# Attention steps emitted in another order

## The chip, the cores and the metric

The kernel runs on one core of a Trainium2 chip. Its time is the device time of one execution in microseconds (us); the span is the part of it between the first and the last recorded instruction. TensorE (PE in the profile) multiplies matrices and, in a queue of its own, loads weights (PEld); VectorE (DVE), ScalarE (ACT) and GpSimd (POOL) work on tiles; SyncE (SP) issues most of the transfers. Each engine runs its own instructions in the order in which the program emits them, and semaphores between engines make it wait.

## The reference

Four batches, eight heads, 768 positions of 64 numbers. Each query and each key is assigned to the nearest of 16 centroids of its head, and attention runs only inside a cluster. The result (3072 tokens of 512) is routed by a greedy choice among eight experts of capacity 384, each a two-layer network:

```
q_assign = argmax(normalize(q) @ normalize(c).T);  k_assign likewise
scores = where(q_assign == k_assign, q @ k.T / 8, -1e9)
x = softmax(scores) @ v
logits = x @ w_gate            # 3072 x 8
# greedy over all (token, expert) pairs by falling logit:
# a token takes an expert that still has room (384 tokens each)
out[tokens of e] = relu(x[tokens of e] @ w1[e]) @ w2[e]
```

## The kernel before

The attention works on eight units, a batch and four heads each; u below is the unit. In a unit there are 24 key tiles s of 128 rows (four heads of six). The steps of a unit, with the lines that record them:

- `load` brings q, k, v (L497, SP). `split_sc`, `split_hi` (ScalarE, L648, L652) and `split_lo` (GpSimd or VectorE, L659, L657) scale a tile and write it as a sum of two half-precision parts. `trans` (L740) has a DMA transpose it. Unit 0 is split and transposed head by head, with `pt` (TensorE, L746) and `ptc` (VectorE L752 or ScalarE L750), which needs no transfer.
- `c0`, `c1`, `c2` to `c4` (L528 to L559) normalise the centroids: squares on VectorE, a root on ScalarE (`c1`, L531), a chain of eleven short VectorE steps, a transpose and a copy. `cent` (L671) multiplies by them, and `hot` or, in unit 0, `hh` (L693 to L709) make a one-of-16 code of the largest product, the last step on ScalarE.
- `m_mm` (L788) and `m_rd` (VectorE, L792) make the maximum of one key tile's scores over a whole row; `row0`, `row1` (GpSimd), `rowt` and `row2` (SP, L813, L817) put the negative maxima into the transposed code of q, so that the score step subtracts them.
- `b_mm` (L827 and L831, four matmuls into one of three score buffers) makes the scores with the cluster term, `b_exp` (ScalarE, L834) their exponentials, and `res` (L842, mostly GpSimd) what the exponential loses in half precision. Four pairs of buffers hold exponentials and residuals.
- `av` (L853 to L859) multiplies exponentials and residuals with v, 18 matmuls, for the six tiles of a head into one accumulator. `out0` to `out2` divide (VectorE, L863 to L877), `hi0` (ScalarE, L885) and `hi1` (VectorE, L889) copy the head out, and the next head's `av` needs the accumulator free. `xst` stores it, `xtr` or, in the last unit's second half, `xpt` and `xpc` transpose it, and `lg0` to `lg2` (L921 to L935) add it to the router's logits.
- `bb,x,i` and `bq,x` (VectorE, L1045 to L1066) start the routing of the first three (x = 0) and the last quarter of the tokens; `bq` writes 128 threshold comparisons (L1063). 86 `tab` steps (mostly GpSimd, L965 to L975) fill small constant tables that only the routing needs. `wd` (L678) is a matmul whose result nobody reads.

All this is written out under a manual schedule: `ATT_ORDER` is a text with one word for each step, and `steps_of` reads it. Steps are emitted in that order; what an engine does first is therefore settled by the text alone, and a step waits only for the buffers and values that it needs. A second text, `FFN_ORDER`, does the same for the experts; the routing between the two texts (L1175 on, with its first decision at L1243) is plain code. The loop is:

```
for name, args in steps_of(ATT_ORDER):
    ...
        norm2[args[0]]()
        hots(int(name[3]), *args)
        hots0(int(name[2]), *args)
        FN[name](*args)
```

Of the kernel before, what the change touches and what calls it, by code (L numbers as in the profile page):

```python
# [26 lines left out]
hh4,0,k zqb split_sc,0,k,3 load,0,v,- split_hi,0,k,1,P split_lo,0,k,1,P pt,0,ka,1 ptc,0,ka,1,D pt,0,qa,3 ptc,0,qa,3,D
pt,0,qa,2 split_hi,0,k,3,P split_lo,0,k,3,P split_hi,0,k,2,P pt,0,ka,3 split_sc,0,v,- split_hi,0,v,-,P zkb ptc,0,qa,2,D
hh5,0,k pt,0,kb,0 ptc,0,ka,3,D ptc,0,kb,0,D cent0,1,k cent0,1,q hh0,1 hh1,1 dup,0,q,0 hh5,0,q dup,0,k,3 pt,0,qb,0
split_lo,0,k,2,P pt,0,ka,2 hh2,1 dup,0,q,1 hh3,1 hh4,1,q dup,0,k,2 hh4,1,k ptc,0,qb,0,A m_mm,0,3 m_rd,0,3 m_mm,0,4  # L30
split_lo,0,v,-,P m_rd,0,4 ptc,0,ka,2,A m_mm,0,5 m_rd,0,5 hh5,1,q dup,0,k,1 load,1,v,- split_sc,1,v,- vs,0 vh2,0 vact,0 vl2,0
load,1,k,- split_sc,1,k,- tab,0 m_mm,0,2 m_rd,0,2 cent0,2,k cent0,2,q hh0,2 hh1,2 tab,31 hh2,2 pt,0,qb,1 ptc,0,qb,1,D
hh5,1,k tab,3 tab,2 hh3,2 hh4,2,k pt,0,kb,1 split_hi,1,k,-,P hh4,2,q zqm split_lo,1,k,-,P m_mm,0,0 m_rd,0,0 m_mm,0,1
m_rd,0,1 ptc,0,kb,1,A dup,0,q,3 hh5,2,k tab,30 dup,0,q,2 m_mm,0,7 load,1,q,- m_rd,0,7 split_sc,1,q,- pt,0,kb,2 ptc,0,kb,2,D
m_mm,0,11 m_rd,0,11 cent0,3,k cent0,3,q hh0,3 row1,0,0 row0,0,0 load,2,k,- pt,0,qm,0 hh5,2,q split_hi,1,q,-,P ptc,0,qm,0,A
trans,1,ka,- pt,0,qb,2 ptc,0,qb,2,A wd hh1,3 m_mm,0,8 m_rd,0,8 hh2,3 m_mm,0,6 m_rd,0,6 hh3,3 hh4,3,k et split_lo,1,q,-,P
trans,1,qa,- b_mm,0,1 b_exp,0,1 res,0,1,P b_mm,0,0 b_exp,0,0 res,0,0,P hh4,3,q hh5,3,k hh5,3,q m_mm,0,15 m_rd,0,15 m_mm,0,10
m_rd,0,10 m_mm,0,13 m_rd,0,13 tab,32 pt,0,kb,3 cent,1,k,0 cent,1,k,2 cent,1,k,1 ptc,0,kb,3,D split_hi,1,v,-,P
split_lo,1,v,-,P cent,1,k,3 hot0,1,k hot1,1,k load,2,q,- hot2,1,k hot3,1,k tab,7 pt,0,qb,3 ptc,0,qb,3,A b_mm,0,4 b_exp,0,4
tab,5 b_mm,0,3 m_mm,0,9 b_exp,0,3 res,0,4,P m_rd,0,9 row0,0,1 b_mm,0,5 b_exp,0,5 row1,0,1 hot4,1,k hot5,1,k m_mm,0,17  # L40
b_mm,0,2 b_exp,0,2 m_mm,0,16 res,0,2,P dup,1,k,- trans,1,kb,- m_rd,0,17 cent,1,q,0 split_hi,2,k,-,D m_rd,0,16 m_mm,0,20
m_rd,0,20 cent,1,q,3 cent,1,q,2 cent,1,q,1 hot0,1,q hot1,1,q pt,0,qm,1 ptc,0,qm,1,A m_mm,0,12 res,0,3,P m_rd,0,12 hot2,1,q
m_mm,0,14 res,0,5,P m_rd,0,14 av,0,0 av,0,1 av,0,2 dup,1,q,- row0,0,2 row1,0,2 b_mm,0,9 b_exp,0,9 hot3,1,q hot4,1,q hot5,1,q
trans,1,qb,- m_mm,0,19 m_rd,0,19 av,0,3 av,0,4 m_mm,0,22 m_rd,0,22 split_lo,2,k,-,D trans,2,ka,- load,2,v,- b_mm,0,10
b_exp,0,10 b_mm,0,7 b_exp,0,7 b_mm,0,6 b_exp,0,6 res,0,6,P m_mm,0,18 m_rd,0,18 av,0,5 out0,0,0 out1,0,0 out2,0,0,D tab,16
b_mm,0,8 b_exp,0,8 res,0,8,P pt,0,qm,2 m_mm,0,23 m_rd,0,23 ptc,0,qm,2,A hi0,0,0 hi1,0,0 vs,1 m_mm,0,21 b_mm,0,11 dup,2,k,-
m_rd,0,21 b_exp,0,11 m_mm,1,7 m_rd,1,7 av,0,6 m_mm,1,13 m_rd,1,13 m_mm,1,8 m_rd,1,8 res,0,7,P av,0,7 m_mm,1,5 m_rd,1,5
row1,0,3 vact,1 vh2,1 res,0,10,P av,0,8 b_mm,0,12 b_exp,0,12 wg0 m_mm,1,0 vl2,1 split_hi,2,q,-,D m_rd,1,0 m_mm,1,4
load,3,k,- m_rd,1,4 res,0,9,P tab,8 tab,9 tab,10 tab,11 tab,12 av,0,9 av,0,10 m_mm,1,1 m_rd,1,1 b_mm,0,14 b_exp,0,14
b_mm,0,15 split_lo,2,q,-,D b_exp,0,15 load,3,v,- row0,0,3 pt,0,qm,3 tab,20 res,0,11,P av,0,11 out0,0,1 res,0,14,P  # L50
ptc,0,qm,3,A m_mm,1,3 m_rd,1,3 res,0,12,P out1,0,1 out2,0,1,D b_mm,0,13 b_exp,0,13 res,0,13,P b_mm,0,17 m_mm,1,2 m_rd,1,2
cent,2,k,0 m_mm,1,11 m_rd,1,11 cent,2,k,1 cent,2,k,2 res,0,15,P wg1 tab,22 trans,2,qa,- b_exp,0,17 res,0,17,P hi0,0,1
cent,2,k,3 hot0,2,k hi1,0,1 xtr,0,0 hot1,2,k b_mm,0,16 b_mm,0,19 m_mm,1,9 m_rd,1,9 b_exp,0,16 res,0,16,P b_exp,0,19 av,0,12
m_mm,1,18 m_rd,1,18 b_mm,0,18 m_mm,1,10 b_exp,0,18 res,0,18,P av,0,13 hot2,2,k m_rd,1,10 wg2 hot3,2,k b_mm,0,21 b_exp,0,21
m_mm,1,12 m_rd,1,12 load,3,q,- m_mm,1,6 m_rd,1,6 row1,1,0 row0,1,0 rowt,1,0 av,0,14 av,0,15 split_hi,2,v,-,D m_mm,1,16
m_rd,1,16 m_mm,1,19 m_rd,1,19 res,0,21,P av,0,16 av,0,17 out0,0,2 b_mm,0,20 b_exp,0,20 hot4,2,k b_mm,0,22 res,0,19,P
res,0,20,P b_exp,0,22 lg0,0,0 out1,0,2 out2,0,2,D hi0,0,2 hot5,2,k lg1,0,0 m_mm,1,15 m_rd,1,15 res,0,22,P xst,0,0 b_mm,0,23
b_exp,0,23 m_mm,1,23 hi1,0,2 cent,2,q,0 cent,2,q,2 cent,2,q,1 cent,2,q,3 m_rd,1,23 hot0,2,q hot1,2,q hot2,2,q hot3,2,q
m_mm,1,14 m_rd,1,14 dup,2,q,- av,0,18 av,0,19 av,0,20 av,0,21 av,0,22 split_hi,3,k,-,D hot4,2,q hot5,2,q res,0,23,P row2,1,0
b_mm,1,2 b_exp,1,2 b_mm,1,3 split_lo,3,k,-,D tab,4 res,1,2,P split_lo,2,v,-,D av,0,23 out0,0,3 out1,0,3 out2,0,3,D b_exp,1,3  # L60
b_mm,1,0 b_exp,1,0 b_mm,1,6 b_exp,1,6 b_mm,1,1 res,1,0,P b_exp,1,1 res,1,1,P m_mm,1,22 m_rd,1,22 vs,2 hi0,0,3 m_mm,1,20
hi1,0,3 m_mm,1,17 trans,2,kb,- dup,3,k,- res,1,3,P m_rd,1,20 split_hi,3,q,-,D b_mm,1,9 av,1,0 av,1,1 b_exp,1,9 trans,2,qb,-
b_mm,1,4 b_exp,1,4 res,1,4,P m_rd,1,17 b_mm,1,5 b_exp,1,5 split_lo,3,q,-,D m_mm,2,1 m_rd,2,1 m_mm,1,21 m_rd,1,21 vact,2
vh2,2 av,1,2 av,1,3 row1,1,1 m_mm,2,0 m_rd,2,0 row0,1,1 b_mm,1,11 b_exp,1,11 xtr,0,1 m_mm,2,4 m_rd,2,4 av,1,4 m_mm,2,2
m_rd,2,2 dup,3,q,- vl2,2 b_mm,1,8 b_exp,1,8 res,1,5,P res,1,6,P res,1,8,P av,1,5 out0,1,0 b_mm,1,10 out1,1,0 out2,1,0,D
b_exp,1,10 res,1,10,P m_mm,2,3 m_rd,2,3 tab,23 m_mm,2,7 m_rd,2,7 trans,3,ka,- cent,3,k,0 cent,3,k,1 b_mm,1,7 m_mm,2,5
hi0,1,0 hi1,1,0 m_rd,2,5 cent,3,k,3 cent,3,k,2 m_mm,2,14 m_rd,2,14 b_exp,1,7 res,1,7,P xst,0,1 av,1,6 m_mm,2,8 m_rd,2,8
rowt,1,1 row2,1,1 b_mm,1,14 b_exp,1,14 m_mm,2,9 m_rd,2,9 av,1,7 hot0,3,k hot1,3,k hot2,3,k hot3,3,k hot4,3,k res,1,9,P
b_mm,1,13 b_exp,1,13 b_mm,1,12 b_exp,1,12 m_mm,2,12 av,1,8 split_hi,3,v,-,D b_mm,1,17 m_rd,2,12 m_mm,2,6 m_rd,2,6 av,1,9
av,1,10 res,1,11,P av,1,11 out0,1,1 out1,1,1 b_exp,1,17 b_mm,1,19 b_exp,1,19 res,1,14,P out2,1,1,D hi0,1,1 m_mm,2,10  # L70
m_rd,2,10 res,1,13,P b_mm,1,16 lg0,0,1 lg1,0,1 tab,26 b_exp,1,16 hi1,1,1 m_mm,2,11 m_rd,2,11 b_mm,1,15 b_exp,1,15
trans,3,qa,- m_mm,2,19 m_rd,2,19 res,1,12,P av,1,12 res,1,19,P m_mm,2,16 b_mm,1,20 m_rd,2,16 load,4,v,- res,1,17,P
b_exp,1,20 m_mm,2,15 av,1,13 m_rd,2,15 m_mm,2,17 load,4,k,- split_hi,4,k,-,D av,1,14 row0,2,0 lg2,0,1 m_mm,2,23 b_mm,1,21
b_exp,1,21 m_rd,2,17 m_rd,2,23 split_lo,3,v,-,D b_mm,1,18 b_exp,1,18 row1,2,0 load,4,q,- hot5,3,k xtr,1,0 lg0,1,0 res,1,15,P
lg1,1,0 lg2,1,0 res,1,16,P av,1,15 av,1,16 av,1,17 res,1,18,P m_mm,2,18 split_hi,4,q,-,D cent,3,q,0 res,1,21,P res,1,20,P
cent,3,q,2 cent,3,q,1 cent,3,q,3 out0,1,2 out1,1,2 out2,1,2,D hi0,1,2 m_rd,2,18 b_mm,1,22 b_exp,1,22 res,1,22,P hot0,3,q
# [1462 lines left out]
```

## Time and profile before

| what | value |
|---|---|
| median of three runs | 678.59 us (677.88 to 680.59) |
| the profiled execution, own time | 678.19 us |
| its span | 676.4 us |
| granted TensorE clock, mean | 0.969 |
| TensorE busy | 637.9 us, 94% |
| GpSimd busy | 512.9 us, 76% |
| VectorE busy | 498.5 us, 74% |
| ScalarE busy | 421.3 us, 62% |

Busy time of TensorE counts matmuls that overlap once. The granted clock is a share of full speed, 1.0 for 2.4 GHz and 0.5 for 1.2. The attention takes the span up to about 371 us, the routing a few microseconds behind it, and the experts the rest.

### The profile page before, as it was taken

What the parts mean: (1) busy time and instruction counts of PE and PEld (TensorE: products, weight loads), DVE (VectorE), ACT (ScalarE), POOL (GpSimd) and SP (SyncE); (2) the same over time, 40 slices, a digit from 0 to 9 for tenths busy, and PEclk for the clock granted to TensorE, in tenths of its full rate; (3) what the DMA queues carried; (4) which work ended last, traced back from release to release, by engine and by line L of the source; (5) the groups of instructions that cost most, each with busy time, mean ns of one, the idle gap of its engine ahead of it and who ended that gap; (6) DMA issues with size and microseconds to landing.
All of it is one profiled execution on the core that took longest, in us unless ns stands there. A gap on an engine that the chain in (4) does not pass through costs nothing. (4 is left out here: it accounts for less than half of the span.)

```text
span 676.4 us, 19511 instructions
## 1 busy us (share of the span) xinstructions
PE 637.9 (94%) x8154; PEld 428.9 (63%) x8154; DVE 498.5 (74%) x1096; ACT 421.3 (62%) x560; POOL 512.9 (76%) x452
## 2 busy tenths in 40 slices
...
GB/s 239 140 144 199 210 156 214 144 149 206 207 115 177 196 143 100 167 73 74 29 51 72 25 234 108 267 105 286 182 209 226 179 222 168 240 302 206 47 1 47
DMA packets 175451, 105.85 MB, mean 156 GB/s; under 512 B 135426, under 2 KB 160002, under 8 KB 175362
## 3 DMA queue, kind: packets, MB, share of 16 engines
...
q14 instruction: 25, 0.20, 0.1%
HBM read 58.77 MB, written 12.58 MB: 105 GB/s over the span
## 5 line engine op out<-in xcount | busy, mean ns | idle before, releaser
L842 POOL TENSOR_TENSOR rt<-pt 128x768 f16<-128x768 f32 x180 | 276.5, 1558 | 26.6 <-ACT pt L834 25.8
L834 ACT ACTIVATE pt<-sc 128x768 f32<-128x768 f32 x192 | 149.8, 811 | 93.9 <-PE sc L831 73.5
L792 DVE TENSOR_REDUCE mxs<-sc 128x1 f32<-128x768 f32 x192 | 176.1, 951 | 17.7 <-PE sc L788 17.2
L1457 PE MATMUL pf<-xgt,w1h 128*128 128x384 f16 (+1 forms) x640 | 130.2, 295 | 0.3 <-DVE xgt L752 0.2
L856 PE MATMUL av<-vh,rt 128*128 128x65 f16 x1152 | 120.6, 193 | 1.7 <-POOL rt L842 1.6
L853 PE MATMUL av<-vh,pt 128*128 128x65 f16 x1152 | 120.7, 194 | 1.1 <-DVE xb L889 1.1
L855 PE MATMUL av<-vl,pt 128*128 128x64 f16 x1152 | 120.4, 191 | 0.0
L855 PEld LDWEIGHTS <-pt 128*128 128x128 bf16 x1152 | 105.8, 98 | 8.6 <-issue 1.5
L853 PEld LDWEIGHTS <-pt 128*128 128x128 bf16 x1152 | 106.2, 97 | 7.3
L856 PEld LDWEIGHTS <-rt 128*128 128x128 f16 x1152 | 105.3, 97 | 1.9 <-POOL rt L842 1.9
L827 PE MATMUL sc<-qbt,kbt 99*128 99x384 f16 x384 | 94.4, 327 | 1.3 <-DVE mxs L792 0.7
L831 PE MATMUL sc<-qat,kat 128*128 128x384 f16 x384 | 94.4, 327 | 0.0
L788 PE MATMUL sc<-kbt,qbt 80*128 80x384 f16 x384 | 90.5, 330 | 2.2 <-DVE qbt L752 0.5
L1457 PE MATMUL pf<-xgt,w1l 128*128 128x384 f16 (+1 forms) x320 | 89.9, 295 | 0.0
L1415 ACT ACTIVATE wr<-wr 128x1024 f32<-128x1024 f32 x64 | 66.7, 1046 | 25.9 <-DMA wr<-in_moe_w_dram 25.3
L1457 PEld LDWEIGHTS <-w1h 128*128 128x128 f16 x640 | 58.0, 98 | 28.3 <-issue 0.9
L1499 PE MATMUL pf<-w2h,hh 128*128 128x512 f16 (+2 forms) x200 | 73.6, 370 | 0.0
L1499 PE MATMUL pf<-w2l,hh 128*128 128x512 f16 (+2 forms) x200 | 73.6, 370 | 0.0
L1499 PE MATMUL pf<-w2h,hl 128*128 128x512 f16 (+2 forms) x200 | 73.2, 370 | 0.0
L1425 POOL TENSOR_TENSOR w2l<-wr,w2h 128x1024 f16<-128x1024 f32 x32 | 67.6, 2133 | 7.3 <-ACT w2h L1418 6.8
L1425 POOL TENSOR_TENSOR w1l<-wr,w1h 128x1024 f16<-128x1024 f32 x32 | 67.4, 2133 | 1.5 <-ACT w1h L1418 1.3
L1489 DVE SCALAR_TENSOR_TENSOR hl<-pf,hh 128x384 f16<-128x384 f32 x56 | 30.9, 553 | 45.7 <-ACT hh L1486 40.2
...
## 6 DMA issues: line engine op xcount, KB each, us to landing
...
xg<-xrow,idx POOLq DMA_INDIRECT x24, 6.5
```

The lines of the kernel that those rows point to most:

```text
L788: nc.tensor.matmul(p[:, half, :S // 2], QBT[u][:D + C, i, :], KBT[u][:D + C, h * J + half * 3:h * J + half * 3 + 3, :], start=True, stop=True)
L792: nc.vector.tensor_reduce(mxs[u % 3][:, i:i + 1], MP.pop((u, i))[:, :, :S // 2], axis=AX.XY, op=OP.max)
L827: nc.tensor.matmul(ps[:, half, :S // 2], KBT[u][:ER + 3, s, :], QBT[u][:ER + 3, cs, :], start=True, stop=False)
L831: nc.tensor.matmul(ps[:, half, :S // 2], KAT[u][:, s, :], QAT[u][:, cs, :], start=False, stop=True)
L834: nc.scalar.activation(pts[(u * 12 + s // 2) % RP][:, s % 2], MP.pop((u, "b", s))[:, :, :S // 2], AF.Exp, scale=ESC)
L842: (nc.vector if e == "D" else nc.gpsimd).tensor_sub(rts[x][:, s % 2], p.rearrange("p a b -> p (a b)"), hi_view(pts[x])[:, s % 2])
L853: nc.tensor.matmul(o[:, j, :D + 1], hi[:, js], VH[u][:, s, :D + 1], start=(kt == 0 and j == 0), stop=False, skip_group_check=True)
L855: nc.tensor.matmul(o[:, j, :D], hi[:, js], VL[u][:, s, :], start=False, stop=False, skip_group_check=True)
L856: nc.tensor.matmul(o[:, j, :D + 1], r[:, js], VH[u][:, s, :D + 1], start=False, stop=(kt == J - 1), skip_group_check=True)
L1425: nc.gpsimd.tensor_sub(lo, wrs[c], hi)
L1457: nc.tensor.matmul(o, (w1l if i == 2 else w1h)[x][:, c, fs], xgt[x][:, h + int(i == 1), ts], start=(first and i == 0), stop=(last and i == ...
L1499: nc.tensor.matmul(PS["o", p, g], (hl if i == 2 else hh)[x][:, f, g * P:(g + 1) * P], (w2l if i == 1 else w2h)[x][:, f, ds], start=(f == 0 ...
```

## The change

The text `ATT_ORDER` is replaced by another one. The words in it are the same, one `wd` excepted, which is gone: 2003 steps for 2004. No function, no buffer and no engine of a step is changed, and `FFN_ORDER` stays. Its first lines and the lines around the last values read:

```
-misc wtio loadc c0 ident c1 c2,0 load,0,k,0 split_sc,0,k,0 c2,1 c2,2 c2,3 c2,4 c2,5 c2,6 split_hi,0,k,0,P load,0,q,0
+load,0,k,3 zqb split_sc,0,k,3 wtio ident loadc c0 c1 load,0,q,1 split_sc,0,q,1 split_hi,0,q,1,P c2,0 c2,1 load,0,q,0
...
-b_exp,7,9 tab,52 b_mm,7,8 res,7,9,D res,7,4,P b_mm,7,10 res,7,2,P av,7,2 b_exp,7,10 av,7,3 av,7,4 res,7,5,P b_mm,7,11 tab,25
+b_mm,7,7 b_exp,7,7 b_mm,7,9 av,7,1 b_exp,7,9 res,7,9,D b_mm,7,10 av,7,2 av,7,3 b_exp,7,10 b_mm,7,11 av,7,4 b_exp,7,11 av,7,5
...
-tab,81 tab,82 tab,68 tab,71 lg1,7,1 lg2,7,1 xst,7,0 xst,7,1 bb,1,0 bb,1,9 bb,1,1 bb,1,2 bb,1,3 bb,1,4 bb,1,5 bb,1,6 bb,1,8
+bb,1,6 bb,1,2 bb,1,9 bb,1,3 bb,1,8 bb,1,10 xst,7,1 bb,1,4 tab,56
```

The first place is the start on ScalarE. `ld` are tiles of unit 0 as loaded, `ss` the centroids' squared lengths. Before:

```order
L531 ACT_TABLE_LOAD
L531 ACTIVATE ss<-ss 128x1
L648 ACTIVATE ld_76<-ld_76 128x384
L652 ACTIVATE ka<-ld_76 128x6x64
L648 ACTIVATE ld_77<-ld_77 128x384
L652 ACTIVATE qa<-ld_77 128x6x64
L648 ACTIVATE ld_77<-ld_77 128x384
```

and after:

```order
L648 ACT_TABLE_LOAD
L648 ACTIVATE ld_76<-ld_76 128x384
L531 ACT_TABLE_LOAD
L531 ACTIVATE ss<-ss 128x1
L648 ACTIVATE ld_77<-ld_77 128x384
L652 ACTIVATE qa<-ld_77 128x6x64
L648 ACTIVATE ld_77<-ld_77 128x384
L652 ACTIVATE qa<-ld_77 128x6x64
```

A tile is scaled ahead of the root, and a table load stands before each of the two.

The second place is VectorE at the first head of unit 7. `xb_148` is that head's copy, `qa` and `offz` belong to `bq`, `ku` and `lo` to `bb`, `rt` are residuals. Before:

```order
L866 RECIPROCAL rc<-rc 128x6
L877 TENSOR_TENSOR av<-av,rc 128x6x64
L1063 TENSOR_TENSOR qa<-bt_99,offz_159 128x768
L889 TENSOR_TENSOR xb_148<-av,xb_148 128x6x64
L1066 TENSOR_SCALAR lo_104<-ku_105 128x18
L842 TENSOR_TENSOR rt_133<-pt_129 128x768
L842 TENSOR_TENSOR rt_134<-pt_130 128x768
```

and after:

```order
L842 TENSOR_TENSOR rt_135<-pt_131 128x768
L842 TENSOR_TENSOR rt_132<-pt_128 128x768
L863 TENSOR_SCALAR rc<-av 128x6
L866 RECIPROCAL rc<-rc 128x6
L877 TENSOR_TENSOR av<-av,rc 128x6x64
L889 TENSOR_TENSOR xb_148<-av,xb_148 128x6x64
L928 TENSOR_REDUCE L<-mx 128x48
L1049 TENSOR_TENSOR eq_100<-eq_100,wt_173 128x144
```

The L1063 step that stood between the division (L877) and the copy (L889) is gone from there.

The third place is VectorE behind the last value step, from the division by L863 to the routing's L1055. `av` is the accumulator, `xb_146` the copy, `xt` its transpose, `mx` and `L` are logits, the others belong to `bb` and `bq`. Before:

```order
L863 TENSOR_SCALAR rc<-av 128x6
L866 RECIPROCAL rc<-rc 128x6
L877 TENSOR_TENSOR av<-av,rc 128x3x64 x2
L1047 TENSOR_TENSOR eq_100<-L,bt_99 128x144
L889 TENSOR_TENSOR xb_146<-av,xb_146 128x3x64 x2
L1049 TENSOR_TENSOR eq_100<-eq_100,wt_173 128x144
L1051 TENSOR_REDUCE m_101<-eq_100 128x18
L752 COPY xt_150<-sc 128x3x128 x2
L1053 TENSOR_TENSOR oh_102<-eq_100,m_101 128x144
L928 TENSOR_REDUCE mx<-mx 128x48
L935 SCALAR_TENSOR_TENSOR L<-mx,L 128x48
L1045 TENSOR_REDUCE bt_99<-L 128x6
```

and after, from the same division on:

```order
L863 TENSOR_SCALAR rc<-av 128x6
L1057 TENSOR_TENSOR ku_105<-bt_99,msk 128x18
L866 RECIPROCAL rc<-rc 128x6
L877 TENSOR_TENSOR av<-av,rc 128x3x64
L1059 TENSOR_SCALAR hs_103<-ku_105 128x18
L877 TENSOR_TENSOR av<-av,rc 128x3x64
L928 TENSOR_REDUCE mx<-mx 128x48
L1053 TENSOR_TENSOR oh_102<-eq_100,m_101 128x144
L935 SCALAR_TENSOR_TENSOR L<-mx,L 128x48
L889 TENSOR_TENSOR xb_146<-av,xb_146 128x3x64 x2
L1063 TENSOR_TENSOR qa<-bt_99,offz_159 128x768
L752 COPY xt_150<-sc 128x3x128 x2
```

Steps of `bb,0` (L1057, L1059, L1053) and of `bq` (L1063) now stand between the division's parts and the copies, where only L1047, L1049 and L1051 stood.

## Rows read from the trace of the kernel before

**Rows 1.** Busy time of each engine (and instructions) by stretch; then granted clock, DMA share, GB/s.

```profile
0.00:24.00 24.00, 13.59 (x169) 10.97 (x170) 15.74 (x43) 20.88 (x37) 17.59 (x40) 1.00 0.74 232
24.00:34.00 10.00, 9.36 (x62) 5.30 (x62) 8.45 (x17) 9.11 (x13) 7.05 (x6) 0.50 0.58 89
...
40.00:300.00 260.00, 256.55 (x4436) 193.83 (x4435) 244.47 (x364) 176.93 (x229) 236.56 (x220) 1.00 0.82 164
300.00:340.00 40.00, 40.00 (x659) 29.84 (x657) 29.50 (x48) 21.80 (x32) 39.59 (x39) 1.00 0.19 44
340.00:370.70 30.70, 27.71 (x568) 21.85 (x565) 22.42 (x36) 16.33 (x24) 23.14 (x33) 1.00 0.32 67
370.70:378.10 7.40, 2.66 (x48) 2.12 (x49) 6.09 (x27) 1.43 (x4) 0.00 (x0) 0.83 0.19 55
378.10:676.40 298.30, 282.25 (x2138) 161.23 (x2137) 166.61 (x559) 170.03 (x216) 182.97 (x114) 0.95 0.53 172
```

**Rows 2.** VectorE's waits, 24 to 40 us: total us, times, longest.

```profile
DVE mxs L792 <- PE sc L788: 2.0, 2, 1.2
```

**Rows 3.** TensorE's waits, 340 to 370 us, in the same columns.

```profile
PE av L856 <- POOL rt L842: 1.6, 1, 1.6
PE av L853 <- DVE xb L889: 1.1, 2, 0.8
```

**Rows 4.** Timeline from 343 to 347 us: start, us, what; idle before.

```profile
343.06 3.60 POOL L842 TENSOR_TENSOR rt<-pt 128x768 f16<-128x768 f32 x2
...
344.29 0.49 PE L827 MATMUL sc<-qbt,kbt 99*128 99x384 f16 x2
...
344.94 0.19 PE L853 MATMUL av<-vh,pt 128*128 128x65 f16 x1
...
346.73 0.20 PE L856 MATMUL av<-vh,rt 128*128 128x65 f16 x1 [1.56 <-POOL rt L842]
```

**Rows 5.** Timeline of ScalarE from 0 us, same columns.

```profile
0.76 1.28 ACT L531 ACT_TABLE_LOAD   x1 [0.76 <-PEq L1525]
2.76 0.20 ACT L531 ACTIVATE ss<-ss 128x1 f32<-128x1 f32 x1 [0.72 <-DVE sq L528]
3.75 0.52 ACT L648 ACTIVATE ld<-ld 128x384 f32<-128x384 f32 x1 [0.79 <-DMA ld<-in_k_dram]
```

**Rows 6.** Timeline of SP's queue and TensorE, 290 to 298 us.

```profile
290.41 3.68 SPq L740 DMA_TRANSPOSE qbt<-qb  x1
...
297.06 0.81 PE L788 MATMUL sc<-kbt,qbt 80*128 80x384 f16 x4
```

**Rows 7.** Timeline of the tail, all engines.

```profile
370.44 0.20 PE L856 MATMUL av<-vh,rt 128*128 128x65 f16 x1
...
371.77 0.30 DVE L1047 TENSOR_TENSOR eq<-L,bt 128x144 bf16<-128x144 f32 x1
...
372.34 1.22 PE L907 MATMUL sc<-ident,xb 128*128 128x128 f16 x12 [1.71 <-ACT xb L885]
...
374.60 0.27 DVE L928 TENSOR_REDUCE mx<-mx 128x48 f32<-128x96 f32 x1 [0.16 <-PE mx L922]
...
375.38 0.96 DVE L1063 TENSOR_TENSOR qa<-bt,offz 128x768 bf16<-128x768 f32 x1
...
378.07 0.17 DVE L1243 TENSOR_SCALAR_CACHE_REDUCE scr<-pc 128x8 bf16<-128x8 f32 x1
```

**Rows 8.** Routing steps by shape group: duration ns min/median/max, first and last start.

```profile
L1057 DVE TENSOR_TENSOR ku<-bt,msk x2: 166/392/619, 335.9 to 377.3; 128x18 int32<-128x18 int32 x1, 128x6 int32<-128x6 int32 x1
...
L1059 DVE TENSOR_SCALAR hs<-ku x2: 171/288/404, 336.6 to 377.5; 128x18 int32<-128x18 int32 x1, 128x6 int32<-128x6 int32 x1
...
L1066 DVE TENSOR_SCALAR lo<-ku x2: 164/566/967, 352.9 to 377.6; 128x18 int32<-128x18 int32 x1, 128x6 int32<-128x6 int32 x1
```

**Rows 9.** Table fills on GpSimd: busy us, mean ns; idle before.

```profile
L975 POOL MEMSET wdb<- 1x128 bf16 x16 | 3.2, 198 | 0.6
```

**Rows 10.** Residuals (L842) on GpSimd: duration ns min/median/max, starts.

```profile
L842 POOL TENSOR_TENSOR rt<-pt x180: 1455/1465/3076, 33.8 to 364.8; 128x768 f16<-128x768 f32 x180
```

More of the change, by code (lines that the diff above doesn't have):

```diff
@@ L27 @@
[L27 to L76, printed above, removed]
@@ new lines @@
+pt,0,kb,1 ptc,0,kb,1,A m_mm,0,2 m_rd,0,2 tab,2 load,1,q,- pt,0,qb,1 ptc,0,qb,1,D load,2,k,- cent0,3,k cent0,3,q hh0,3 tab,26
+tab,31 m_mm,0,1 zqm m_rd,0,1 m_mm,0,0 m_rd,0,0 row1,0,0 row0,0,0 dup,0,q,2 m_mm,0,7 m_rd,0,7 trans,1,ka,- hh5,2,k pt,0,kb,2
+ptc,0,kb,2,D hh5,2,q m_mm,0,11 m_rd,0,11 pt,0,qm,0 split_sc,1,q,- split_hi,1,q,-,P split_lo,1,q,-,P m_mm,0,8 et hh1,3
+ptc,0,qm,0,A pt,0,qb,2 ptc,0,qb,2,A m_rd,0,8 hh2,3 m_mm,0,6 m_rd,0,6 b_mm,0,0 tab,9 b_exp,0,0 hh3,3 m_mm,0,10 hh4,3,q
+hh5,3,q hh4,3,k b_mm,0,1 b_exp,0,1 m_rd,0,10 m_mm,0,15 m_rd,0,15 res,0,0,P cent,1,k,0 cent,1,k,2 m_mm,0,13 m_rd,0,13
@@ new lines @@
+split_sc,1,v,- b_mm,0,4 tab,30 res,0,1,P m_mm,0,9 m_rd,0,9 row0,0,1 trans,1,qa,- cent,1,k,1 cent,1,k,3 hot0,1,k hh5,3,k
+pt,0,kb,3 b_exp,0,4 ptc,0,kb,3,D tab,7 dup,1,k,- av,0,0 res,0,4,P m_mm,0,17 m_rd,0,17 pt,0,qb,3 ptc,0,qb,3,A hot1,1,k
+row1,0,1 hot2,1,k b_mm,0,5 b_exp,0,5 hot3,1,k hot4,1,k b_mm,0,3 b_exp,0,3 tab,54 tab,8 b_mm,0,2 b_exp,0,2 tab,12 tab,24
+m_mm,0,16 m_rd,0,16 m_mm,0,22 loadg hot5,1,k m_rd,0,22 cent,1,q,0 cent,1,q,3 tab,76 cent,1,q,2 load,2,v,- cent,1,q,1
+load,2,q,- m_mm,0,12 hot0,1,q hot1,1,q split_hi,1,v,-,P pt,0,qm,1 ptc,0,qm,1,A res,0,5,P split_hi,2,k,-,D hot2,1,q hot3,1,q
@@ new lines @@
+dup,1,q,- av,0,1 res,0,2,P res,0,3,P av,0,2 av,0,3 av,0,4 trans,1,kb,- m_rd,0,12 split_lo,1,v,-,P hot4,1,q m_mm,0,20
+m_rd,0,20 hot5,1,q trans,1,qb,- av,0,5 out0,0,0 b_mm,0,6 b_exp,0,6 res,0,6,P b_mm,0,9 b_exp,0,9 m_mm,0,19 split_lo,2,k,-,D
+tab,64 m_rd,0,19 vs,1 vact,1 m_mm,0,14 b_mm,0,7 b_exp,0,7 trans,2,ka,- m_rd,0,14 row0,0,2 out1,0,0 m_mm,0,23 m_rd,0,23
+b_mm,0,10 b_exp,0,10 out2,0,0,D hi0,0,0 m_mm,0,18 m_rd,0,18 load,3,k,- b_mm,0,8 m_mm,0,21 m_rd,0,21 row1,0,2 pt,0,qm,2
+b_exp,0,8 ptc,0,qm,2,A vh2,1 hi1,0,0 m_mm,1,13 m_rd,1,13 b_mm,0,11 b_exp,0,11 m_mm,1,7 m_rd,1,7 dup,2,k,- tab,81 av,0,6
@@ new lines @@
+m_mm,1,8 tab,3 m_rd,1,8 tab,69 m_mm,1,4 m_rd,1,4 res,0,7,P wg0 res,0,8,P av,0,7 m_mm,1,5 m_rd,1,5 b_mm,0,14 m_mm,1,0
+m_rd,1,0 res,0,10,P b_exp,0,14 av,0,8 m_mm,1,3 m_rd,1,3 split_hi,2,q,-,D b_mm,0,15 res,0,9,P av,0,9 row0,0,3 b_exp,0,15
+tab,10 b_mm,0,12 load,3,q,- split_lo,2,q,-,D b_exp,0,12 m_mm,1,1 m_rd,1,1 row1,0,3 pt,0,qm,3 load,3,v,- ptc,0,qm,3,A
+split_hi,3,k,-,D vl2,1 res,0,11,P av,0,10 av,0,11 out0,0,1 m_mm,1,2 res,0,12,P res,0,14,P m_rd,1,2 out1,0,1 wg1 trans,2,qa,-
+b_mm,0,13 m_mm,1,11 cent,2,k,0 m_rd,1,11 tab,50 cent,2,k,1 b_exp,0,13 cent,2,k,2 out2,0,1,D hi0,0,1 m_mm,1,9 m_rd,1,9
@@ new lines @@
+m_rd,2,11 m_mm,2,16 m_rd,2,16 lg1,0,1 lg2,0,1 res,1,14,P res,1,17,P av,1,13 av,1,14 b_exp,1,18 m_mm,2,18 m_rd,2,18
+trans,3,qa,- res,1,15,P dup,3,q,- split_hi,4,q,-,D m_mm,2,23 m_rd,2,23 m_mm,2,17 m_rd,2,17 xtr,1,0 lg0,1,0 av,1,15 b_mm,1,21
+res,1,16,P av,1,16 av,1,17 lg1,1,0 lg2,1,0 out0,1,2 out1,1,2 out2,1,2,D m_mm,2,15 b_exp,1,21 m_rd,2,15 hi0,1,2 b_mm,1,23
+row0,2,0 hi1,1,2 b_exp,1,23 cent,3,q,0 cent,3,q,2 cent,3,q,1 cent,3,q,3 row1,2,0 b_mm,1,22 b_exp,1,22 hot0,3,q hot1,3,q
+res,1,19,P hot2,3,q res,1,18,P av,1,18 rowt,2,0 row2,2,0 hot3,3,q b_mm,2,0 b_exp,2,0 hot4,3,q hot5,3,q m_mm,2,21 m_rd,2,21
@@ new lines @@
+trans,3,kb,- av,1,19 m_mm,2,13 m_rd,2,13 trans,3,qb,- m_mm,2,22 m_rd,2,22 vs,3 split_hi,4,k,-,D split_lo,4,k,-,D vh2,3
+vact,3 trans,4,ka,- res,1,20,P res,1,21,P av,1,20 av,1,21 b_mm,2,2 b_exp,2,2 split_lo,4,q,-,D b_mm,2,4 b_exp,2,4 res,1,23,P
+m_mm,2,20 res,1,22,P av,1,22 av,1,23 b_mm,2,3 res,2,0,P res,2,2,P b_exp,2,3 m_rd,2,20 row0,2,1 row1,2,1 rowt,2,1 out0,1,3
+out1,1,3 b_mm,2,6 b_exp,2,6 out2,1,3,D hi0,1,3 m_mm,3,3 load,5,k,- m_rd,3,3 b_mm,2,1 m_mm,3,4 m_rd,3,4 b_exp,2,1 m_mm,3,7
+m_rd,3,7 b_mm,2,7 m_mm,3,8 m_rd,3,8 hi1,1,3 b_exp,2,7 res,2,4,P res,2,1,P b_mm,2,5 b_exp,2,5 m_mm,3,2 m_rd,3,2 xst,1,0
```

232 lines of the change are left out of this document (126 added, 106 removed).

## Prediction

> **What bounds the kernel now.** The page's busy shares mix stages, so I read the busy time of each engine by stretches of the span first [rows 1]. From 40 to 300 us TensorE is busy 256.55 of 260 us and from 300 to 340 all 40.00; VectorE (244.47 of 260) and, from 300 to 340, GpSimd (39.59 of 40) are nearly as full. There an order can only move idle time that is hardly there. TensorE has idle time in three places: at the start (24.00 − 13.59 = 10.4, then 0.6 by 34 us), from 340 to 370.7 (2.99), and after 370.7, the tail between the last value matmul and the routing (4.74 of 7.40). The work from 378.1 on is emitted from the other table, which is the same text.
>
> The early idle time does not set the end by itself. VectorE makes the cluster codes and the row maxima there, and from 24 to 34 us it is busy 8.45 of 10. From 24 to 34 us TensorE's granted clock is 0.50, the 1.2 GHz level, and its matmuls take longer; yet in the stretch from 24 to 40 us the trace puts only 2.0 us of VectorE's waiting on them [rows 2]. So even a full clock there would return about 2 us, not half of 10.
>
> From 340 us on two of TensorE's waits are named [rows 3]: 1.6 us for a residual from GpSimd (L856 behind L842) and 1.1 us for the free accumulator (L853 behind L889). In single rows [rows 4]: a matmul of `av,7,2` starts at 346.73 after 1.56 us of idle; its residual is the second of two residuals after 343.06, which take 3.60 us together.
>
> **The change part by part.** The 2004 steps become 2003: one dummy matmul is gone, every other step is there, on the same engine. So no duration is added but one: an ACT_TABLE_LOAD. I take the four regions in turn, against the profiled execution's own 678.19 us.
>
> *Start.* Today ScalarE loads the table at 0.76 us (1.28 us), waits for the centroids' squares and runs the root at 2.76; its first scaling follows at 3.75, when k's tile has landed [rows 5]. In the new order one scaling stands ahead of the root, with a load of its own, and the root with a second load behind it. The centroid load goes second on SP's queue. The root can then start only after 3.75 + 0.52 + 1.28 = 5.55 us instead of 2.76: 2.8 us later. Its reader is the first cluster matmul of head 0, which comes behind a dozen small VectorE steps; VectorE's hand-off to it moves by some 1.5 us after what those steps can give back. Against that, fewer code and reduction steps of later heads stand before the sixth row maximum. Added in order with the same rows' durations, the fourteenth maximum ends about 0.3 us earlier than today. I take −0.3 us. Bounds: +1.5 if the table load and its delay stay on VectorE's chain whole, −2.0 if VectorE's waits in the slow stretch [rows 2] vanish.
>
> The Trainium skill, ScalarE: Activation LUTs, section "Table sets: the hidden batching unit", says to batch activations by set, since functions of different sets cost a load at each change; the order here breaks that rule once. It names 1.283 us for a load in "What ACT_TABLE_LOAD costs", and the row's 1.28 agrees. By the rule alone the start would be 1.3 us worse; by the rows most of it lies beside VectorE's other work, and I keep −0.3.
>
> *Middle (40 to 340 us).* TensorE's whole idle time here is 260 − 256.55 = 3.45 us [rows 1], the most that could be gained. New waits are possible where the list leaves less room. One of them: the transposed code of unit 7 (`trans,7,qb`). Today it starts on SP's queue at 290.41 and its first reader at 297.06, 6.65 us later [rows 6]. In the new list TensorE has between the step that makes this code and the first reader six score steps of four matmuls, two max steps of two, and one value step of 18. A score step lasts 0.65 us (344.29 to 344.94 in [rows 4]), a max step half of that, and matmuls of a value step start 0.03 us apart: 6 × 0.65 + 2 × 0.33 + 18 × 0.03 = 5.1 us. So up to 1.5 us are missing if the producer ends where it is listed. The maxima's rows (row0 to b_mm) of units 1, 2, 3, 4 and 5 are tightened likewise. SP's queue runs in order, so a late row holds the transposes behind it. I take 0, because VectorE and TensorE are already full, and keep −3.45 and +2.5 for the range.
>
> *End (340 to 370.7).* New: `res,7,3` stands behind `res,7,1`, `res,7,4` and `res,7,2`, and four score steps stand between `av,7,0` and `av,7,2` where two did. The wait of 1.56 us should go. The copy-out of head 0 (`hi1,7,0`) no longer stands behind the 0.96 us offset step (L1063) on VectorE, so most of the accumulator's 1.1 us goes. Late next: `av,7,17`, whose residual `res,7,17` comes on VectorE behind the routing step `bb,0,5`; I price that wait like that step's neighbour L1057, at most 0.62 us [rows 8], and take 0.5. Net of 2.7 named and 0.5 new: −2.2 us. The logits of unit 7's first half (12 small matmuls, 0.03 us apart) now follow the last value matmul, and the dummy is gone: −0.4 us of TensorE before it, some of it hidden today. Bounds for the region: 0 (new waits eat all) to −3.0 (all idle gone).
>
> *Tail.* Today the last value matmul ends at 370.64 and VectorE follows it step by step [rows 7]; among them only four routing steps of the first half, at 0.30 us or less each, some 1.1 us. In the new order `bq,1` goes ahead of the last value step, and behind it stand 0.62 (L1057), 0.40 (L1059), 0.30 (L1053, priced as L1047), 0.96 (L1063) and 0.97 us (L1066), 3.25 in all, and the first half's last logit reduction (0.27) and its sum (some 0.2): 2.6 us more [rows 7, 8]. What stands between the two normalising steps of the last head (0.62 + 0.40) is on the path; the 0.96 and 0.97 lie beside the transposes (1.22 us from 372.34) and the logit matmuls behind them. The count waits for `bb,1,4`, now last of its group, so four steps, of about 0.17 us at this size [rows 8] and today behind it, come ahead. By adding in order the first routing decision (L1243, today at 378.07) comes 8.45 us after the last value matmul instead of 7.4: +1.0 us. Bounds 0 (all of it in holes) and +2.6 (none).
>
> *FFN.* Same instructions, same order: 0. A shift of the start can move where the clock falls, which I leave at ±1 us, an estimate from the 0.95 mean clock of the last stretch [rows 1].
>
> Sum: −0.3 + 0 − 2.2 − 0.4 + 1.0 = −1.9 us, 676.3 us against the profiled 678.19. The median of the three runs is 678.59, 0.4 above; I keep 676.3.
>
> **The rivals.**
> Faster than that. The slow stretch at 24 to 34 us does not return, because the new order has more score work earlier in unit 0, and VectorE's 2.0 us come back; the middle gives half of its 3.45. Then −1.9 − 2.0 − 1.7 = 672.6 us. For it: VectorE waits only for TensorE there. Against it: TensorE still has little to do between 18 and 24 us, as today.
>
> Slower: GpSimd becomes late. 86 small table steps fill GpSimd's holes; today 64 of them stand before `av,7,0`, in the new order 82. 18 more at 0.2 us [rows 9] are 3.6 us. From 300 to 340 us GpSimd has 0.41 us of idle [rows 1] and feeds every value step. If the residuals are late by more than the new lead of the score steps, TensorE waits 3.6 us; with the tail's +1.0 and the start's +0.5 it is 678.19 + 5.1 = 683.3. Against it: until 300 us GpSimd has 23.4 us free, and most of the moved steps stand there. It decides as soon as residual waits before 340 us exceed 1 us in sum.
>
> The Trainium skill, SBUF — State Buffer, section "SBUF: two separate sides", says that GpSimd and VectorE share one port pair under an exclusive lock, so that one blocks while the other holds it. The trace agrees as far as it shows it: a residual takes 1.465 us in the median on GpSimd and 3.076 at most [rows 10]. By that rule the end would lose again what residuals on VectorE gain there; no price above rests on it.
>
> No effect: the order moves waits that TensorE and VectorE hide anyway, the end's gain is spent in the tail: 678.2 us. For it stands the 40.00 of 40 us; against it the two waits in the last stretch, which have no cover.
>
> **How the numbers follow.** About 0.5% (3.4 us) is what a measurement of this kernel can tell from no change: faster is below 675.2, slower above 682.0. Forecast (674 to 679) 0.42, of which 0.13 below 675.2; the faster rival 0.23; no effect 0.19; the slower rival 0.16. So faster 0.36, same 0.47, slower 0.17. The likeliest case alone reaches from 674 to 679. To hold 8 in 10 the range takes in the start's and middle's lower bounds in part (671) and the slower rival's near end (683).
>
> **What would show it.** The changed profile should have no residual wait above 0.6 us after 340 us (end step), L1243 about 8.4 us after the last value matmul (tail), a second table load before 6 us with the fourteenth row maximum ending near 37 us (start), and TensorE busy at least 256 of 260 us from 40 to 300 (middle). The forecast is wrong if TensorE waits for SP's transposes of unit 7, if GpSimd residuals are waited for before 340 us, or if the slow clock leaves 24 to 34 us and the last value matmul ends before 366 us.

## The result: 0.7% slower, and one VectorE step that GpSimd keeps out

The changed kernel took 683.41 us in the median of five runs (681.75 to 685.86), the kernel before 678.87 (677.88 to 680.59). The ratio is 1.0074 with a 95% interval of 1.0045 to 1.0103. 676.3 us was forecast, with a range to 683.0. The profiled execution took 682.36 us with a span of 680.6, against 678.19 and 676.4.

The busy time of each engine by stretches of the changed kernel answers to [rows 1]; the columns are the same.

```profile
0.00:24.00 24.00, 12.90 (x161) 10.28 (x161) 14.08 (x40) 20.84 (x37) 16.89 (x39) 1.00 0.65 200
24.00:34.00 10.00, 8.49 (x65) 4.94 (x64) 9.44 (x18) 8.03 (x13) 7.94 (x9) 0.61 0.68 160
40.00:300.00 260.00, 257.88 (x4408) 193.52 (x4405) 245.30 (x364) 180.36 (x232) 240.61 (x234) 1.00 0.82 164
300.00:332.00 32.00, 32.00 (x544) 24.30 (x542) 25.45 (x37) 15.85 (x23) 31.59 (x32) 1.00 0.23 41
332.00:336.50 4.50, 0.06 (x1) 0.00 (x0) 4.50 (x3) 0.81 (x1) 2.77 (x2) 1.00 0.40 89
336.50:341.00 4.50, 4.49 (x18) 2.24 (x18) 3.07 (x6) 2.34 (x4) 2.45 (x2) 0.62 0.00 0
341.00:374.70 33.70, 33.41 (x694) 26.76 (x693) 21.26 (x39) 19.63 (x28) 20.55 (x20) 1.00 0.28 63
374.70:382.20 7.50, 2.91 (x61) 2.32 (x58) 6.36 (x30) 1.53 (x4) 0.00 (x0) 0.71 0.19 55
382.20:680.60 298.40, 280.85 (x2138) 160.91 (x2137) 166.58 (x559) 170.18 (x216) 182.93 (x114) 0.96 0.53 172
```

From 332 to 336.5 us TensorE stands still, in a stretch where before it was busy 40.00 of 40 us. VectorE is busy all of that time, and behind the stop TensorE's granted clock falls (0.62 in the mean of 336.5 to 341, so partly at 1.2 GHz). From 341 us on TensorE is busy 33.41 of 33.70 us; the idle time of the old end has gone.

The waits of TensorE from 300 us to the last value matmul are, in the columns of [rows 3]:

```profile
PE sc L827 <- DVE mxs L792: 4.4, 1, 4.4
PE av L853 <- DVE xb L889: 0.3, 1, 0.3
```

Both waits of [rows 3] are mended (2.7 us before, 0.3 now), and one of 4.4 us is new: a score step needs a score buffer that a row maximum on VectorE still has to read. The timelines of VectorE and of GpSimd show why that maximum is late (start, duration, what).

```profile
327.80 0.29 DVE L1045 TENSOR_REDUCE bt<-L 128x18 f32<-128x144 f32 x1
328.12 7.47 DVE L1063 TENSOR_TENSOR qa<-bt,offz 128x768 bf16<-128x768 f32 x1
335.51 1.81 DVE L792 TENSOR_REDUCE mxs<-sc 128x1 f32<-128x768 f32 x2
```

```profile
327.47 2.88 POOL L842 TENSOR_TENSOR rt<-pt 128x768 f16<-128x768 f32 x2
330.30 0.19 POOL L975 MEMSET wdb<- 32x128 bf16 x1
330.47 4.30 POOL L842 TENSOR_TENSOR rt<-pt 128x768 f16<-128x768 f32 x3
```

L1063 is the comparison of `bq,2`, which took 0.96 us at 375.38 in [rows 7]. Here it takes 7.47. GpSimd runs five residuals and a table fill without a break from 327.47 to 334.77, and L1063 ends 0.82 us after the last of them. It is recorded as running, so no list of waits names it. The two row maxima behind it, `m_rd,7,18` and `m_rd,7,19`, wait with it, TensorE waits for them, and GpSimd comes to its end only because TensorE's stop leaves it without exponentials.

Where the 4.2 us of the two spans lie, from the ends of the same steps in both traces:

| stretch | before | after | difference | forecast |
|---|---|---|---|---|
| start to the end of `av,6,17` | 331.46 | 331.41 | −0.1 | −0.3 |
| to the end of unit 6, `av,6,23` | 8.39 | 15.25 | +6.9 | 0 |
| to the last value matmul | 30.78 | 28.06 | −2.7 | −2.6 |
| to the first routing decision, L1243 | 7.44 | 7.52 | +0.1 | +1.0 |
| rest | 298.33 | 298.36 | 0 | 0 |

The order also moves work over these borders: in the new one a score step (0.65 us) more stands in the second stretch and one more in the third, both taken from ahead of `av,6,17`. So not all of the +6.9 is L1063's. With L1063 elsewhere and the rest of the new order as it is (the step in a hole, below), the second stretch takes 9.28 us, which leaves 6.0 us for L1063.

### The profile page after: what moved, and what is told of

Its sections match the earlier page's. It is cut to its first block, busy times and chain, and to the rows that moved or that the text cites. A ratio compares the mean times of both kernels' runs of the same rounds, so it can differ in the third digit from the quotient of the medians.

```text
span 680.6 us, 19509 instructions
## 1 busy us (share of the span) xinstructions
PE 639.0 (94%) x8153; PEld 429.3 (63%) x8153; DVE 500.6 (74%) x1096; ACT 423.8 (62%) x561; POOL 508.9 (75%) x452
## 5 line engine op out<-in xcount | busy, mean ns | idle before, releaser
L842 POOL TENSOR_TENSOR rt<-pt 128x768 f16<-128x768 f32 x180 | 271.9, 1531 | 31.1 <-ACT pt L834 27.8
L792 DVE TENSOR_REDUCE mxs<-sc 128x1 f32<-128x768 f32 x192 | 177.2, 949 | 17.8 <-PE sc L788 17.0
L788 PE MATMUL sc<-kbt,qbt 80*128 80x384 f16 x384 | 92.0, 334 | 0.4 <-DMA qbt<-qb 0.2
```

Of the source, the lines that this page charges most:

```text
L788: nc.tensor.matmul(p[:, half, :S // 2], QBT[u][:D + C, i, :], KBT[u][:D + C, h * J + half * 3:h * J + half * 3 + 3, :], start=True, stop=True)
L792: nc.vector.tensor_reduce(mxs[u % 3][:, i:i + 1], MP.pop((u, i))[:, :, :S // 2], axis=AX.XY, op=OP.max)
L842: (nc.vector if e == "D" else nc.gpsimd).tensor_sub(rts[x][:, s % 2], p.rearrange("p a b -> p (a b)"), hi_view(pts[x])[:, s % 2])
```

## The experiments

Theory 1 was that L1063 is kept out by GpSimd's residuals and that this alone makes the kernel slower. Theory 2 was that the loss is spread over the start, the tail and a fuller GpSimd, and only shows at that place.

**The step put back where it stood.**

```diff
-bb,0,0 bq,2 m_mm,7,18 m_rd,7,18
+bb,0,0 m_mm,7,18 m_rd,7,18
...
-out2,7,0,D xtr,6,1
+out2,7,0,D bq,2 xtr,6,1
```

> The changed kernel with one step moved: bq,2 (L1063) goes back to where it stands before the change, behind the division of unit 7's head 0. Theory 1 (the offset step is shut out by GpSimd's residuals, holds the two row maxima behind it and so TensorE's score buffers): TensorE's 4.45 us wait for L792 at 332 to 336.5 us goes, and the stretch at half clock behind it (336.5 to 341) goes too; in place of it some of the accumulator's wait returns, up to 1 us. Time 675.5 to 677.5. Theory 2 (the loss is spread: the second table load, the tail, a fuller GpSimd; the wait is only where the slack shows): the idle time moves to another step and the time stays at 681 or more.

Measured: 678.10 us against 679.95 of the kernel before in the same session, ratio 0.9979 (0.9955 to 1.0002). L1063 takes 1.89 us, and TensorE's waits from 300 us on are:

```profile
PE av L853 <- DVE xb L889: 1.0, 2, 0.7
PE sc L827 <- DMA qbt<-mt: 0.3, 1, 0.3
```

The 4.4 us are gone and did not come back elsewhere, so theory 2 falls. The accumulator's 1.0 us has returned, as was said; the absolute time is 0.6 us above the expected range, in a session in which the kernel before was 1.1 us longer as well.

**The step moved by two VectorE instructions**, behind both row maxima, with GpSimd's rows untouched.

```diff
-bq,2 m_mm,7,18 m_rd,7,18 av,6,15 m_mm,7,19 m_rd,7,19
+m_mm,7,18 m_rd,7,18 av,6,15 m_mm,7,19 m_rd,7,19 bq,2
```

> The changed kernel with bq,2 (L1063) moved by two VectorE instructions, behind the row maxima of m_rd,7,18 and m_rd,7,19; GpSimd's rows are the same. Theory 1: L1063 still takes over 3 us, since GpSimd's residuals run on without a break and now TensorE is not stopped by the missing score buffers; what waits is the division of unit 6's head 2 behind it, so TensorE waits for the accumulator (L853 behind L889) by 2 us or more. Time 678 to 682. Rival (L1063 was long for a reason of its own place, the values it reads): it takes about 1 us here and the time falls to 676.

Measured: 684.55 us, ratio 1.0070 (1.0048 to 1.0092). VectorE, GpSimd and TensorE's longest wait:

```profile
331.94 7.24 DVE L1063 TENSOR_TENSOR qa<-bt,offz 128x768 bf16<-128x768 f32 x1
```

```profile
331.21 7.16 POOL L842 TENSOR_TENSOR rt<-pt 128x768 f16<-128x768 f32 x5
```

```profile
PE sc L788 <- DVE mxs L792: 4.9, 1, 4.9
```

As long as before at another time and behind other instructions: the step's own place is not the reason. What waits was named wrongly: a later row maximum, not the division; and the time lies above the expected 678 to 682.

**One residual left out**, `res,6,17`. A gap of 0.33 us opens on GpSimd.

```diff
-res,6,17,P
```

> The changed kernel without one residual on GpSimd, res,6,17 (its value step then uses an older residual, so a part of the computation is left out). bq,2 stands where the change puts it. GpSimd then has to wait some 0.3 us for the exponential of tile 19 right after L1063 has started. Theory 1: L1063 gets in at that gap and takes under 2.5 us instead of 7.47; TensorE's wait for L792 falls from 4.45 to under 0.5 us; time about 676. Rival (L1063 is long by itself there): still over 6 us, and time 681 or more.

Measured: 678.32 us in one run. The two engines:

```profile
329.47 1.62 DVE L1063 TENSOR_TENSOR qa<-bt,offz 128x768 bf16<-128x768 f32 x1
```

```profile
328.82 1.46 POOL L842 TENSOR_TENSOR rt<-pt 128x768 f16<-128x768 f32 x1
330.22 0.19 POOL L975 MEMSET wdb<- 32x128 bf16 x1
330.75 3.09 POOL L842 TENSOR_TENSOR rt<-pt 128x768 f16<-128x768 f32 x2 [0.33 <-ACT pt L834]
```

L1063 stands where the change puts it and waits for one residual (to 330.28) instead of five. GpSimd's run without a break is what made it long, and TensorE does not wait for L792 here. The time is that of a single run, 2 us above the expected 676.

**The same step early in the kernel before.**

```diff
-m_rd,7,18 m_rd,7,14
+bb,0,0 bq,2 m_rd,7,18 m_rd,7,14
...
-bb,0,0 bb,0,5
+bb,0,5
...
-b_exp,7,11 bq,2 b_mm,7,12
+b_exp,7,11 b_mm,7,12
```

> The kernel before the change with bq,2 and the step it needs (bb,0,0) moved ahead of the row maximum m_rd,7,18, the place they have in the changed kernel. Theory 1: L1063 meets back-to-back residuals (GpSimd is busy 39.59 of 40 us there), takes 2 to 7 us, and TensorE waits for L792 or, behind it, the division; time 680 to 684 against 678.9. Theory 2: nothing but one VectorE step of 0.95 us is moved in a stretch where VectorE has idle time, and the time stays within 0.7 us of the kernel before.

Measured: 681.22 us, ratio 1.0014 (0.9991 to 1.0036): no change that can be told. L1063 ran beside two residuals that followed each other at once, and took 1.04 us:

```profile
328.24 1.04 DVE L1063 TENSOR_TENSOR qa<-bt,offz 128x768 bf16<-128x768 f32 x1
```

```profile
327.00 3.61 POOL L842 TENSOR_TENSOR rt<-pt 128x768 f16<-128x768 f32 x2
```

Here VectorE got in at the seam, and the second residual paid (3.61 us for two, where two take 2.88 above). The expectation of theory 1 failed: a neighbour that runs on is needed for the loss, and is not always enough.

**The step moved by one VectorE instruction.**

```diff
-bq,2 m_mm,7,18 m_rd,7,18
+m_mm,7,18 m_rd,7,18 bq,2
```

> The changed kernel with bq,2 moved by a single VectorE instruction, behind the row maximum m_rd,7,18; GpSimd's rows are unchanged. By the run before it, L1063 then asks at about 331.0 us, when one residual on GpSimd has just ended and a table fill stands before the next. Theory 1a (it is shut out by any run of residuals that goes on): again over 5 us and about 684 us. Theory 1b (it is shut out only if it asks in the middle of a residual that another follows at once; asking at the seam it gets in): about 1 to 1.3 us, TensorE's wait for L792 under 0.5 us, and 677 to 679 us.

Measured: 685.66 us in one run; L1063 asked at 332.39 us, just when a residual had ended, and took 6.64 us, with 5.2 us of TensorE's wait behind it.

```profile
332.39 6.64 DVE L1063 TENSOR_TENSOR qa<-bt,offz 128x768 bf16<-128x768 f32 x1
```

So 1b fell. What lets it in at one seam and not at another stays open.

**The same kernel once more.**

> The changed kernel once more, unaltered. If L1063's 7.47 us is a matter of chance between executions it is short here, under 3 us, and the time is near 677; if it follows from the order of the two engines it is again 6.5 to 7.5 us, TensorE's wait for L792 is 4 to 5 us, and the time 681 to 686.

Measured: 685.39 us, L1063 7.50 us, TensorE's wait for L792 4.5 us.

```profile
329.96 7.50 DVE L1063 TENSOR_TENSOR qa<-bt,offz 128x768 bf16<-128x768 f32 x1
```

In five executions (two of this kernel, the two moved versions and the one below) it took 6.6 to 7.5 us; it is the order, not chance.

**Another form of the comparison, in the same place.**

```diff
+        for t in range(x * J, (x + 1) * J) if x == 2 else ():
+            nc.vector.tensor_scalar(ind0[:, t], offs0[0], bt0[:, t:t + 1], None, op0=OP.is_le)
```

> The changed kernel with its order unaltered; only the comparison of bq,2 is written in another form: six instructions, one for each group of tokens, that compare the thresholds (one tensor operand of 128 numbers) with one number in each partition, instead of one instruction with two tensor operands. If the second tensor operand is what GpSimd's residuals shut out, the six take under 0.4 us each, TensorE's wait for L792 is under 0.6 us and the time is 676.5 to 679 us. Rival (any VectorE instruction that reads only SBUF is shut out there): the first of the six takes 5 to 7 us and the time stays at 682 to 686 us.

Measured: 683.93 us, ratio 1.0063 (1.0037 to 1.0088). The line of the six, with durations in ns as min/median/max:

```profile
L1070 DVE TENSOR_SCALAR qa<-offz,bt x6: 274/274/6733, 332.2 to 339.6; 128x128 bf16<-128x128 f32 x6
```

The first takes 6.73 us, the rest 0.27 each. The second tensor operand is not what matters. The Trainium skill, SBUF — State Buffer, section "Who interferes with whom", names both kinds: VectorE instructions with two inputs in SBUF, and copies and `tensor_scalar` in a two-port mode, contend with GpSimd, and whichever comes second is blocked until the first is done. The runs agree that both forms are kept out (in which mode the six ran, the trace does not say); they differ in that VectorE stays out for four or five GpSimd instructions in a row, not for one.

**The step in a hole of both engines**, behind the last row maximum, at the end of GpSimd's run of residuals.

```diff
-bb,0,0 bq,2 m_mm,7,18
+bb,0,0 m_mm,7,18
...
-m_rd,7,22 m_rd,7,21 row1,7,1
+m_rd,7,22 m_rd,7,21 bq,2 row1,7,1
```

> The changed kernel with bq,2 behind m_rd,7,21, where VectorE waits some 2 us for the next value steps and GpSimd waits for the two row maxima. Theory 1: L1063 takes under 1.5 us, neither TensorE's wait for L792 (4.45 us) nor the accumulator's wait of the run with bq,2 put back (1.0 us) is there; 1 us less than that run, 676.5 to 678 us against 679.9 of the kernel before. Theory 2 (the loss is spread): 681 us or more.

Measured: 676.69 us against 678.72, ratio 0.9974 (0.9956 to 0.9991): faster than both kernels. VectorE's step and TensorE's only wait from 300 us to the last value matmul:

```profile
338.68 1.59 DVE L1063 TENSOR_TENSOR qa<-bt,offz 128x768 bf16<-128x768 f32 x1
```

```profile
PE av L853 <- DVE xb L889: 0.3, 1, 0.3
```

GpSimd was not idle yet, and L1063 was kept out here too: the last residual of the run ended at 339.46, and L1063 0.81 us later.

```profile
338.00 1.46 POOL L842 TENSOR_TENSOR rt<-pt 128x768 f16<-128x768 f32 x1
```

But no residual followed that one at once, and TensorE's only wait is the 0.3 us above.

**And the root ahead of the first scaling.**

```diff
-load,0,k,3 zqb split_sc,0,k,3 wtio ident loadc c0 c1
+loadc load,0,k,3 wtio ident c0 c1 zqb split_sc,0,k,3
```

> The kernel with bq,2 in the hole, and the centroids' root ahead of the first scaling, their load first on SP's queue: one table load less on ScalarE, rows as before the change. If the second table load is what makes unit 0's row maxima 1.5 to 2 us later than in the kernel before, they come 1.5 us earlier, and as TensorE is full from 40 to 330 us the end comes 1 to 1.5 us earlier too. If the delay is taken up by VectorE's and TensorE's idle time, as the prediction had it, the time stays within 0.5 us of the kernel with bq,2 in the hole.

Measured: 676.16 us, ratio 0.9971 (0.9954 to 0.9988), 0.5 us below the version with the step in the hole alone, which the two intervals do not tell from no gain. The second table load of 1.28 us is gone, but unit 0's row maxima do not come earlier: the thirteenth on VectorE ends at 39.94 us (39.65 in the next version, which lacks that load too), and at 39.07 in the version with the step in the hole. So in this kernel, which also loads k's tile behind the centroids, the second load is not what makes them late. That idle time takes the delay up, as the prediction had it, is not shown by this run.

**And the tail's four steps later.**

```diff
-bb,1,5 bb,1,1 bb,1,6 bb,1,2 bb,1,9 bb,1,3 bb,1,8 bb,1,10 xst,7,1 bb,1,4
+bb,1,1 bb,1,2 bb,1,9 bb,1,3 xst,7,1 bb,1,4 bb,1,5 bb,1,6 bb,1,8 bb,1,10
```

> The kernel of the run before with four routing steps of the last quarter (L1055, L1057, L1059, L1066) put behind the step that the first count waits for (L1053). They take 0.17 us each without GpSimd beside them; the first decision L1243 comes 0.3 to 0.6 us earlier, and the time is 0.3 to 0.6 us less. With all of it, 675 to 677.5 us, the fastest of these kernels. Rival: the count waits for something else (the comparisons of L1063) and nothing changes.

Measured: 676.82 us, ratio 0.9986 (0.9965 to 1.0007). No gain: the step L1053 ends only 0.1 us sooner behind the last value matmul, since the comparison of 0.95 us stands before it in both, and the four steps now come between it and L1243 on VectorE. L1243 comes 7.93 us behind the last value matmul, for 7.49 in the version before.

**Dummy matmuls in unit 0**, on top of the version with the step in the hole.

```diff
-m_mm,0,5 cent0,2,k
+m_mm,0,5 wd wd wd cent0,2,k
...
+wd (16 more, behind pt and m_mm steps that TensorE idles after)
```

> The kernel with bq,2 in the hole and 19 more dummy matmuls (wd, L678) in TensorE's idle time of unit 0, from 14 to 33 us. In the profiles so far TensorE's granted clock is 0.5 for 7 to 17 us after 24 to 30 us, of a length that differs between executions, and the executions whose stretch is longest are 3 us longer. If the clock is what spreads the executions and TensorE's idle time ahead of it is what lowers the clock, the stretch at 0.5 goes or starts after 33 us, av,0,23 comes 1 to 3 us earlier than 89 us, and the time is 674.5 to 676.5 us with less spread. Rival (VectorE sets the pace of unit 0 and hides the low clock): the time stays within 0.7 us of the kernel with bq,2 in the hole. If the dummies come in the way of unit 0's steps, it is up to 2 us slower.

Measured: 677.38 us against 679.22, ratio 0.9964 (0.9951 to 0.9978), no better than without them. TensorE's row from 24 to 46 us, first of the version in the hole, then of a second one (the root's), then with the dummies:

```profile
24.00:46.00 22.00, 18.73 (x232) 11.90 (x231) 19.65 (x34) 17.92 (x26) 16.50 (x23) 0.84 0.71 176
```

```profile
24.00:46.00 22.00, 19.82 (x177) 12.22 (x176) 17.34 (x31) 15.56 (x22) 13.84 (x21) 0.61 0.72 176
```

```profile
24.00:46.00 22.00, 20.47 (x304) 14.04 (x300) 21.00 (x38) 19.93 (x28) 17.87 (x24) 1.00 0.87 185
```

The clock (0.84, 0.61, 1.00) does what was expected of it, and the last value matmul comes 1.4 us earlier than in the hole's version (367.76 for 369.15). The expected time was missed: the routing gives the 1.4 us back, as the first expert's matmul starts at 401.7 us in both, and the experts end another 1.4 us later (span 676.3 for 674.9). From 390 to 402 us TensorE's mean clock is 0.64 here and 0.78 in the hole's version; whether that is the reason was not tested.

## Why the prediction was wrong

*The step that failed* is the sentence that no duration is added but one. The middle was priced at 0, with +2.5 at most, from TensorE's idle time and SP's transfers. For `bq,2` the working told only what it leaves behind at unit 7's head, and not where it goes: directly ahead of two row maxima that TensorE soon needs, beside GpSimd's fullest stretch (39.59 of 40 us in [rows 1]). That place cost 6.0 us (15.25 us for the stretch, 9.28 with the step in the hole): 4.45 us of standstill, and most of the rest behind it, where the mean clock was 0.62 for 4.5 us.

The 0.96 us that the prediction gives this step is that of another quarter's comparison on the same line [rows 7]. The `bq,2` that was moved took twice that in the kernel before, beside a residual (VectorE, then GpSimd):

```profile
350.58 1.96 DVE L1063 TENSOR_TENSOR qa<-bt,offz 128x768 bf16<-128x768 f32 x1
```

```profile
350.26 1.46 POOL L842 TENSOR_TENSOR rt<-pt 128x768 f16<-128x768 f32 x1
```

It ended 0.82 us after that residual, as it ended 0.82 us after the last of five in the changed kernel.

*The rule of the Trainium skill* on the shared ports (SBUF — State Buffer, section "SBUF: two separate sides") was weighed and then put aside with the remark that no price rests on it. The price that was left out lies there. The rows to take it from were there: 3.076 us for a residual of 1.465 [rows 10], and in [rows 8] steps of 0.16 us that took 0.62, 0.40 and 0.97. These were read as the cost of their larger shape. In the changed kernel, where GpSimd is idle beside them, the same shapes take 0.17 us:

```profile
L1057 DVE TENSOR_TENSOR ku<-bt,msk x2: 165/167/169, 374.8 to 380.3; 128x18 int32<-128x18 int32 x1, 128x6 int32<-128x6 int32 x1
L1059 DVE TENSOR_SCALAR hs<-ku x2: 160/164/168, 375.5 to 381.5; 128x18 int32<-128x18 int32 x1, 128x6 int32<-128x6 int32 x1
L1066 DVE TENSOR_SCALAR lo<-ku x2: 162/163/164, 378.8 to 381.5; 128x18 int32<-128x18 int32 x1, 128x6 int32<-128x6 int32 x1
```

*The tail* was therefore sized wrongly too, +1.0 us for a measured +0.1: the three steps cost 0.5 us together, not 2.0.

*The end* was right in mechanism: the residual's wait of 1.56 us and most of the accumulator's 1.1 us went, and the new wait of 0.5 us at `av,7,17` did not come. That −2.7 us stands against −2.6 is partly luck: TensorE's idle time in the stretch fell by 2.6 us and not by 2.2, and the 0.4 us of moved matmuls were nearly made up by the score step that came in.

*The start* was near in its sum and not in its parts. The root runs at 5.05 us instead of 2.76. The row maximum that the prediction calls the fourteenth (tile 13's, the thirteenth on VectorE) ends 1.5 us later, at 38.9 for 37.4 us, the bound, and not 0.3 us earlier; the one behind it ends 1.1 us earlier (39.9 for 40.9). The second table load alone does not explain it, since the two kernels without that load have tile 13's maximum no earlier (39.9 and 39.7 us); the cause stays open. TensorE's idle time from 40 to 300 us shrank from 3.45 to 2.12 us, and at the end of `av,6,17` both kernels are level, with two score steps fewer done in the new order.

*The rivals.* The slower one gave 683.3 us, near the measured time, for a wrong reason: TensorE never waits for a residual before 340 us, and the table steps in GpSimd's holes cost nothing that shows. The faster rival's condition failed: the half clock came back at 24 to 34 us (0.61 in the mean). The third rival, no effect, failed too, as the time moved up by more than its interval. And none of the prediction's three signs of being wrong came (no long wait for the transposes of unit 7, none for a residual before 340 us, and the slow clock stayed where it was): two watched other waits and one the clock, and the loss began inside a recorded duration.

Without the kept-out step the sum comes out, and its terms less well. The version with it in the hole is 2.0 us faster than the kernel before, and 1.9 was worked out. In the two profiles it is +0.4 us to the end of `av,6,17`, −1.8 from there to the last value matmul, +0.1 in the tail and −0.2 behind it, against −0.3, −2.6, +1.0 and 0: misses that cancel in part.
